# Two transformer layers on one core: feature sums on TensorE, small products on GpSimd, a first chunk normalised tile by tile, and an order written out as a table

## The chip, the cores and the metric

The kernel is one program on one core of a Trainium2 chip. A core has TensorE (matrix products; PE in the profile, and PEld for its weight loads), VectorE (DVE), ScalarE (ACT), GpSimd (POOL) and SyncE (SP), which run their own instruction streams in order and wait for each other by semaphores. In this kernel SyncE and, at the start, ScalarE issue the DMA transfers. The metric is the device time of one execution in microseconds. Lower is better.

## The reference

A sequence of 2048 rows of 512 bfloat16 values goes through an attention layer (A) and a gated feed-forward layer (B), twice, with the same weights both times:

```python
def _A_ref(x, wqkv, w_phi, wo):            # H = 32 heads of Dh = 16
    q, k, v = ...                          # from x @ wqkv
    pq = jnp.einsum("bhsd,hdf->bhsf", q, w_phi)
    pk = jnp.einsum("bhsd,hdf->bhsf", k, w_phi)
    phi_q = jnp.concatenate([_softmax(pq), _softmax(-pq)], axis=-1)
    phi_k = jnp.concatenate([_softmax(pk), _softmax(-pk)], axis=-1)
    kv = jnp.einsum("bhsf,bhsd->bhfd", phi_k, v)
    z  = jnp.einsum("bhsf->bhf", phi_k)
    num = jnp.einsum("bhqf,bhfd->bhqd", phi_q, kv)
    den = jnp.einsum("bhqf,bhf->bhq", phi_q, z)[..., None] + 1e-6
    return (num / den) ... @ wo
def _B_ref(x, W_gate, W_up, W_down):       # F = 1376
    gate, up = x @ W_gate, x @ W_up
    return ((gate * (gate > 0)) * up) @ W_down
x = x + _A_ref(_layernorm(x), ...)
x = x + _B_ref(_layernorm(x), ...)         # and both once more
```

The attention is linear: keys and values are first summed over all 2048 rows into one small matrix for each head, and only then can the queries be applied.

## The kernel before

The 2048 rows are 16 tiles of 128, in four chunks of four tiles. X stays in the core's memory for the whole run. For each chunk and layer the stages are these.

**Normalisation** (class `Norm`, line 367). The statistics of a tile come either from VectorE (`bn_stats` at L385, aggregated at L387), or from sums: the addition that makes the new X also accumulates its row sum (L494), and ScalarE accumulates the squares (L408). GpSimd makes the inverse standard deviation with a few tiny instructions (L393 to L444). ScalarE (L456), VectorE or GpSimd (both L468) scales the tile. The scaled tile is then transposed, either by a DMA transpose that SyncE issues, one tile at a time (L486) or a pair of tiles (L482), or on TensorE (L477) with a copy out of PSUM (L304 on ScalarE, L306 on VectorE). `groups` says how many tiles share the tiny instructions; for the first chunk it is (1, 1, 2), and `turn` ("A---") has tile 0 alone turned on TensorE.

**Weights of the features** (`feature_weights`). `w_phi` is folded into the key and query weights: the key weights are transposed on TensorE (L348), multiplied (L361) and copied out (L304, L306); the query weights are transposed by two DMA transposes (L334).

**Keys and values** (`keys_values`, `values`). For each tile four matmuls give the features (L637) and four the values (L590). ScalarE takes exp of the features and of their negatives (L642). `feature_sums` adds up each head's 16 exponentials of either sign: in one VectorE reduction (L609), in two halves (L619), or with a first addition on GpSimd (L606) and the rest on VectorE (L615). VectorE inverts the sums (L651); GpSimd, VectorE or both multiply (L657); eight matmuls of 68 columns add the tile into the key-value sums (L679). VectorE then spreads those sums into the matrix R (L701).

**Queries and attention** (`queries`, `attention`). Four matmuls (L721), two exps (L725), the sums as above, a reciprocal (L730) and a small product (L732), both on VectorE, a scale of half of the tile (L739), a DMA transpose (L741), eight matmuls against R (L758), a division (L776, L778), a transpose (DMA at L785 and L791, or TensorE at L798) and the output projection (L809).

**Feed-forward** (`glu`). For each chunk matmuls with the gate and the up weights (L540, and L520 for the last 96 columns), evacuation by ScalarE and VectorE, and eleven matmuls for each tile of the result (L572). Other weights than those of keys, values and queries are loaded by SyncE, piece by piece (`load_weights`, L297).

The **order** on every engine is made when the program is built. Each operation is recorded with an engine, a duration and what it reads and writes (`Plan.op`); loads carry an earliest time (`at`), which is known to the planner only. `Plan.order` then goes through a planned time and gives each free engine the ready operation with the highest rank, which is the longest chain behind it plus a bias from the table `RANK`. Operations are emitted in that order, and at run time each engine keeps to it, waiting on semaphores for data and for buffers. There are six PSUM buffers of the kind `ps` (`KINDS`). Strings in `STEP`, one letter per tile, choose among the variants: `kr` and `qr` the way of the feature sums for keys and queries ("1" one reduction, "2" two, "P" and "H" with GpSimd), `qs` and `ks` who scales, `xn`, `xB` and `xA` who normalises, `ev` who evacuates values, with the layer behind the name.

Of the kernel before, what the change touches and what calls it, by code (L numbers as in the profile page):

```python
# [60 lines left out]
class Plan:  # L61
# [10 lines left out]
    def op(self, eng, occ, fn, reads=(), writes=(), holds=(), lat=0.0, at=0.0, group=None, port=False, long=False):  # L72
# [4 lines left out]
        base, slope = RANK.get(f"{o.group}.{eng}") or RANK[o.group]  # L77
        o.bias = base - slope * o.i_in
# [19 lines left out]
    def order(self):  # L98
        for o in self.ops:
            for p in o.preds:  # L100
                p.succs.append(o)
        for o in reversed(self.ops):
            o.rank = o.cost + o.lat + max([s.rank + hop(o.eng, s.eng) for s in o.succs], default=0.0)
        free = {k: [0.0] * n for k, (pool, n) in self.kinds.items()}
        engines = sorted({o.eng for o in self.ops})
        busy = {e: 0.0 for e in engines}
        ready = {e: [] for e in engines}
        for o in self.ops:
            o.wait, o.t0 = len(o.preds), o.at
            if not o.wait:  # L110
                ready[o.eng].append(o)
        seq, left, now, shut = [], len(self.ops), 0.0, 0.0
        while left:
            moved, later = False, []
            for e in engines:
                if busy[e] > now + 1e-9:
                    later.append(busy[e])
                    continue
                best = None
                for o in ready[e]:  # L120
                    if o.t0 > now + 1e-9:
                        later.append(o.t0)
                        continue
                    if o.port and shut > now + 1e-9:
                        later.append(shut)
                        continue
                    ok = True
                    need = {}
                    for b in o.bufs:
                        if b.slot is None:  # L130
                            need[b.kind] = need.get(b.kind, 0) + 1
                    for k, n in need.items():
                        got = [t for t in free[k] if t is not None]
                        if len(got) < n:
                            ok = False
                        else:
                            t = sorted(got)[n - 1]
                            if t > now + 1e-9:
                                later.append(t)
                                ok = False  # L140
# [792 lines left out]
```

## Time and profile before

| | |
|---|---|
| median of three runs | 382.85 us (381.29 to 383.61) |
| the profiled execution | 380.87 us |
| its span, first to last instruction | 379.1 us |
| TensorE busy | 368.0 us, 97%, 2435 matmuls |
| VectorE, ScalarE, GpSimd busy | 272.1, 211.0 and 139.5 us |
| mean granted clock of TensorE | 0.995 |

The times of instructions come from one profiled execution, which has a time of its own; the median is that of three others. A matmul's busy time includes the time that its result takes to drain, so consecutive matmuls overlap: four of 512 columns take about 0.86 us when others follow. In a timeline row the columns are the start and the length in us, the engine and line, the operation, output and inputs, and in brackets the engine's idle time before it and what ended it. In a row of groups stand the busy time in us and the mean of one in ns, then the idle time before them. In the table by stretches each engine has its busy us and its instructions; PEclk is the granted clock as a share of full speed, then the busy share of the DMA engines and GB/s. A row of the DMA view gives an issue's count, size and us from issue to landing.

### The profile page before, as it was taken

The page shows a single profiled execution, that of the slowest core. Times are in us where ns is not written, and L with a number is a line of the kernel's source. Part 1 is how long each engine was busy: PE and PEld are TensorE (multiplying, and loading weights), DVE is VectorE, ACT ScalarE, POOL GpSimd, SP SyncE. Part 2 cuts the span into 40 slices and gives each one's busy share as a digit, 9 for nine tenths or more (in the row PEclk, how much of TensorE's full clock was granted, in tenths as well). Part 3 has the DMA queues.
Part 4 walks back from the last instruction along what each step waited for, and adds up shares of the span by engine and source line. Part 5 has one row for each costly group of instructions (what it writes and reads, how often), then busy time and mean ns, then how long its engine had stood idle before and what let it go on. Part 6 is the DMA issues. An engine that isn't in the chain of part 4 may idle for free.

```text
span 379.1 us, 6873 instructions
## 1 busy us (share of the span) xinstructions
PE 368.0 (97%) x2435; PEld 190.8 (50%) x2435; DVE 272.1 (72%) x606; ACT 211.0 (56%) x436; POOL 139.5 (37%) x272
## 2 busy tenths in 40 slices
PE   8699999999999999999999999999999999999996
PEld 4245545666445454444454455576655444454444
DVE  5999999999789725636992688999985592532232
ACT  4899878752598241238476377986725135124600
POOL 3799876903366000134360446545311021000000
PEclk9899999999999999999999999999999999999999
DMA  8999816449585100141232020656977014020011
GB/s 255 252 219 212 211 39 138 47 91 173 96 153 100 29 15 2 28 57 29 47 52 55 3 55 2 124 104 86 164 153 112 0 28 112 0 28 30 1 43 55
DMA packets 98403, 32.23 MB, mean 85 GB/s; under 512 B 88800, under 2 KB 98368, under 8 KB 98368
## 3 DMA queue, kind: packets, MB, share of 16 engines
q1 hardware_dynamic: 94400, 28.36, 39.8%
q10 hardware_dynamic: 3968, 3.42, 2.9%
q8 instruction: 19, 0.31, 0.4%
q14 instruction: 16, 0.13, 0.1%
HBM read 8.44 MB, written 2.10 MB: 28 GB/s over the span
## 4 chain that ended last, share of the span: by engine, by line
PE 80%; DVE 9%; DMA 4%; POOL 4%; issue 1%; SPq 1%; ACT 0%; ACTq 0%; POOLq 0%
PE ps L540 36%; PE ps L572 19%; PE ps L809 6%; PE ps L721 4%; PE ps L590 4%; PE ps L637 3%; DMA b<-b 3%; PE ps L520 3%; PE q L758 2%; DVE sk L619 2%; POOL b L657 1%; PE ps L315 1%; DVE rk L651 1%; PE q L679 1%; DVE bnst L385 1%
## 5 line engine op out<-in xcount | busy, mean ns | idle before, releaser
L540 PE MATMUL ps<-b,wu 128*128 128x512 bf16 (+2 forms) x400 | 79.4, 337 | 0.0
L540 PE MATMUL ps<-b,wg 128*128 128x512 bf16 (+2 forms) x400 | 78.9, 337 | 0.0
L572 PE MATMUL ps<-wd,b 128*128 128x512 bf16 (+3 forms) x374 | 78.3, 367 | 0.0
L550 ACT CAST b<-ps 128x512 bf16<-128x512 f32 (+2 forms) x100 | 48.9, 505 | 40.6 <-PE ps L540 39.3
L553 DVE SCALAR_TENSOR_TENSOR b<-ps,b 128x512 bf16<-128x512 f32 (+2 forms) x60 | 34.9, 598 | 30.3 <-PE ps L540 29.8
L572 PEld LDWEIGHTS <-b 128*128 128x128 bf16 (+1 forms) x374 | 35.3, 98 | 39.4
L657 POOL TENSOR_TENSOR b<-b,rk 128x1024 bf16<-128x1024 bf16 (+6 forms) x30 | 42.1, 1410 | 33.9 <-DVE rk L651 26.0
L540 PEld LDWEIGHTS <-wg 128*128 128x128 bf16 x400 | 36.2, 98 | 32.9 <-issue 0.2
L540 PEld LDWEIGHTS <-wu 128*128 128x128 bf16 x400 | 36.1, 98 | 31.9
L456 ACT ACTIVATE b<-X,ve,rstd 128x512 bf16<-128x512 bf16 x42 | 33.4, 818 | 26.2 <-POOL ve L444 21.5
L739 POOL TENSOR_TENSOR b<-b,rq 128x512 bf16<-128x512 bf16 x25 | 26.3, 1050 | 31.2 <-DVE rq L732 24.2
L498 DVE TENSOR_TENSOR X<-X,ps 128x512 bf16<-128x512 bf16 (+2 forms) x34 | 22.0, 649 | 21.2 <-PE ps L572 20.6
L725 ACT ACTIVATE b<-ps 128x512 bf16<-128x512 f32 x64 | 33.3, 615 | 6.2 <-PE ps L721 6.1
L408 ACT ACTIVATE sq<-X 128x512 bf16<-128x512 bf16 x32 | 20.0, 626 | 28.5 <-DVE X L494 26.2
L637 PE MATMUL ps<-Wk,b 128*128 128x512 bf16 x128 | 31.5, 388 | 4.0 <-DMA b<-b 4.0
L642 ACT ACTIVATE b<-ps 128x512 bf16<-128x512 f32 x64 | 33.2, 612 | 1.2 <-PE ps L637 1.2
L494 DVE SCALAR_TENSOR_TENSOR X<-ps,X 128x512 bf16<-128x512 f32 x32 | 21.7, 684 | 13.4 <-PE ps L572 12.5
L809 PE MATMUL ps<-wo,b 128*128 128x512 bf16 x128 | 30.9, 379 | 0.1
L590 PE MATMUL ps<-wkv,b 128*128 128x512 bf16 x128 | 30.9, 384 | 0.0
L721 PE MATMUL ps<-Wq,b 128*128 128x512 bf16 x128 | 30.9, 379 | 0.0
L557 DVE TENSOR_TENSOR b<-b,b 128x512 bf16<-128x512 bf16 (+2 forms) x40 | 14.1, 373 | 22.3 <-ACT b L550 21.9
L546 ACT ACTIVATE b<-ps 128x512 bf16<-128x512 f32 (+2 forms) x40 | 19.8, 496 | 15.1 <-PE ps L540 15.1
(84 smaller groups left out, 463.8 us busy)
## 6 DMA issues: line engine op xcount, KB each, us to landing
out_dram<-X SPq DMA_DIRECT2D x15, 128.0 KB, 1.7
X<-in_A_x_dram ACTq DMA_DIRECT2D x3, 512.0 KB, 7.6
b<-b SPq DMA_TRANSPOSE x87, 3.2
wd<-in_B_W_down_dram SPq DMA_DIRECT2D x5, 256.0 KB, 3.2
wu<-in_B_W_up_dram SPq DMA_DIRECT2D x8, 160.0 KB, 3.3
wg<-in_B_W_gate_dram SPq DMA_DIRECT2D x8, 160.0 KB, 2.9
wkv<-in_A_wqkv_dram ACTq DMA_DIRECT2D x2, 512.0 KB, 5.1
wq<-in_A_wqkv_dram ACTq DMA_DIRECT2D x1, 512.0 KB, 8.3
```

Of the source, the lines that this page charges most:

```text
L456: pl.op("ACT", 0.72, lambda to=to, t=t, j=j: nc.scalar.activation(out=to(), in_=st.X[:, t, :], func=AF.Identity, scale=rstd[:, j:j + 1], b ...
L540: nc.tensor.matmul(ps[:], lhsT=wt[:, b, f * P:(f + 1) * P], rhs=xnT[:, lo:hi, b, :], start=(b == 0), stop=(b == NDB - 1))
L550: pl.op("ACT", 0.065 + 0.42 * share, lambda ups=ups, ru=ru: nc.scalar.copy(out=ru[:], in_=ups[:]), reads=[(ups, 0)], writes=[(ru, 0)])
L553: pl.op("DVE", 0.08 + 0.53 * share, lambda gps=gps, ru=ru, h=h, cs=cs: nc.vector.scalar_tensor_tensor(out=h[:, cs], in0=gps[:], scalar=0.0 ...
L572: nc.tensor.matmul(yps[:], lhsT=hs[f][:fsz, ti * P:(ti + 1) * P], rhs=st.wd[:fsz, f, cols], start=(f == 0), stop=(f == NFT - 1))
L590: nc.tensor.matmul(vp[:], lhsT=xnT[:, ti, kb, :], rhs=st.wkv[:, kb, D:2 * D], start=(kb == 0), stop=(kb == NDB - 1))
L637: nc.tensor.matmul(ps[:], lhsT=xnT[:, ti, kb, :], rhs=w(kb), start=(kb == 0), stop=(kb == NDB - 1))
L642: pl.op("ACT", 0.49, lambda s=s, ek=ek, pk=pk: nc.scalar.activation(out=ek[:, :, s, :], in_=pk[:].rearrange("p (j x) -> p j x", j=8), func ...
L657: eng.tensor_tensor(out=phiK[:, lo:hi, :, :].rearrange("p j s (f h) -> p (j s) f h", h=4), in0=ek[:, lo:hi, :, :].rearrange("p j s (f h) - ...
L721: nc.tensor.matmul(pq[:], lhsT=xnT[:, ti, kb, :], rhs=st.Wq2[:, kb, :], start=(kb == 0), stop=(kb == NDB - 1))
L725: pl.op("ACT", 0.49, lambda s=s, eq=eq, pq=pq: nc.scalar.activation(out=eq[:, :, s, :], in_=pq[:].rearrange("p (j x) -> p j x", j=8), func ...
L809: nc.tensor.matmul(yps[:], lhsT=turned(b), rhs=st.wo[:, b, :], start=(b == 0), stop=(b == NDB - 1))
```

## The change

1. `feature_sums` gets a way "T". The tile of exponentials is transposed by a DMA transpose on SyncE, and eight matmuls with a 0/1 matrix of eight columns (`M8s`) add up its features into PSUM. The reciprocal then reads PSUM. The table uses it for key tiles 0, 2, 4, 6, 9 and 11 of the first layer.
2. A string `qm` says for each query tile whether the small product runs on VectorE or GpSimd; 20 of 32 are on GpSimd.
3. The first chunk is normalised in groups (1, 1, 1, 1), and `turn` is "ADDD": all four tiles are transposed on TensorE, and VectorE copies three of them out.
4. Other strings of `STEP` change: who scales, evacuates and normalises, which chunks take their statistics from sums, which tiles are transposed in pairs. In the second layer's B stage three tiles of a chunk were turned on TensorE, now one.
5. `Plan.order` no longer searches. It reads the order of all 1891 operations from the table `ORDER`, and `RANK` goes. Some planned durations and arrival times are changed; they have no effect at run time but through that table.

The computed function stays the same. The diff, cut to its core:

```diff
     def order(self):
-        ... (the search by rank)
         free = {k: [0.0] * n for k, (pool, n) in self.kinds.items()}
+        busy, shut, seen = {}, 0.0, set()
+        assert sorted(ORDER) == list(range(len(self.ops)))
+        self.seq = [self.ops[i] for i in ORDER]
+        for o in self.seq:
+            assert o.preds <= seen
+            seen.add(o)
...
-WF_IN, WK_IN, WV_IN, WQ_IN, LOADED = 3.5, 5.9, 8.6, 13.1, 13.0
-X_IN = [3.25, 3.8] + [7.0] * 2 + [10.1] * 4 + [11.6] * 4 + [14.5] * 4
+WF_IN, WK_IN, WV_IN, WQ_IN, LOADED = 3.4, 6.05, 8.25, 12.75, 13.0
+X_IN = [3.25, 4.55] + [6.75] * 2 + [9.75] * 4 + [11.25] * 4 + [14.2] * 4
...
+    st.M8s = const.tile([P, 2, 4], BF16, name="M8s")
+    nc.vector.tensor_reduce(out=st.M8s[:], in_=ident[:].rearrange("p (z k h) -> p z h k", z=2, h=4), axis=AX.X, op=Alu.max)
...
+    if how == "T":
+        turned = Buf("b2", [P, 8, P], BF16)
+        pl.op("SP", 1.25, lambda: nc.sync.dma_start_transpose(out=turned[:], in_=e[:].rearrange("p j s x -> p (j s x)")),
+              reads=[(e, 0), (e, 1)], writes=[(turned, 0)], lat=2.0, group=(group, t))
+
+        def add_up():
+            for j in range(8):
+                nc.tensor.matmul(sums[:, j, :, :].rearrange("p s h -> p (s h)"), lhsT=turned[:, j, :],
+                                 rhs=st.M8s[:].rearrange("p s h -> p (s h)"), start=True, stop=True)
+        pl.op("PE", 0.26, add_up, reads=[(turned, 0)], writes=[(sums, 0), (sums, 1)], group=(group, t))
+        return
...
+        how = STEP["qr" + L][t]
+        sums = Buf("ps", [P, 8, 2, 4], F32) if how == "T" else sq2
+        feature_sums(st, how, eq, sums, "f" + L, "i" + L, t)
...
+        by_pool = STEP["qm" + L][t] == "P" and how != "T"
+        pl.op("POOL" if by_pool else "DVE", 0.23 if by_pool else 0.19, lambda sq2=sq2, sums=sums, rq=rq, by_pool=by_pool: (
+            nc.gpsimd if by_pool else nc.vector).tensor_tensor(out=rq[:], in0=sq2[:, :, 1, :], in1=sums[:, :, 0, :], op=Alu.mult),
+            reads=[(sq2, 1), (sums, 0)], writes=[(rq, 0)])
...
-    "part0": "4111", "part1": "4111", "tB0": "A---", "tB1": "D-DA", "tA": "----", "wev": "AADDAAADADAAAAAA",
+    "part0": "4111", "part1": "4111", "tB0": "A---", "tB1": "---A", "tA": "----", "wev": "AAADDAADAADDAAAA",
...
-    "xn1": "AAAAADAPDAADAADA", "turn": "A---", "wake": 17, ..., "sB0": 3, "sB1": 2, "sA": 3,
+    "xn1": "DADDADAPDAADAADA", "turn": "ADDD", "wake": 19, ..., "sB0": 4, "sB1": 4, "sA": 2,
...
-    "kr0": "H1111P1121221222", "kr1": "P12111111H12P222",
+    "kr0": "T1T1TPT12T1T1222", "kr1": "12P121211222P221", "qm0": "DDDDPPPPPDPPPPDP", "qm1": "PDDPDPPDPPPPDPPD",
...
-RANK = {...}
+ORDER = (
+    128, 129, 142, 137, 139, 125, 140, 133, 132, 135, 136, 130, 126, 127, 143, 0, 1, 2, 3, 144, 7, 4, 8, 145, 5,
...
-        n = Norm(st, "b4", (1, 1, 2) if c == 0 else (2, 2), STEP["xn1"], STEP["xm0"], X_IN, STEP["turn"] if c == 0 else "")
+        n = Norm(st, "b4", (1, 1, 1, 1) if c == 0 else (2, 2), STEP["xn1"], STEP["xm0"], X_IN, STEP["turn"] if c == 0 else "")
```

In the program built from the changed kernel, SyncE's first instructions are the two loads of X, one load each of up, gate and down weights, the transpose for tile 0's sums, the transpose of the tile pair 4 and 5, another load, a transpose of query weights, the pair 6 and 7, the other transpose of query weights, and the transpose for tile 2's sums. In the kernel before they are the two loads of X, the transpose of tile 1, a load of down weights, the pair 2 and 3, the pair 4 and 5, and the two of query weights.

127 lines of the change are left out of this document (30 added, 97 removed), and 125 rows, old and new, of tables (ORDER, RANK, STEP).

## The prediction

> **What bounds the kernel now.** I read the page's totals first, then the table by stretches, then the TensorE timeline of the start, then the chain of waits of the first layer.
>
> ```profile
> span 379.1 us, 6873 instructions
> PE 368.0 (97%) x2435; PEld 190.8 (50%) x2435; DVE 272.1 (72%) x606; ACT 211.0 (56%) x436; POOL 139.5 (37%) x272
> ```
> ```profile
> core 0: us, PE busy (x) PEld busy (x) DVE busy (x) ACT busy (x) POOL busy (x), PEclk, DMA share, GB/s
> 0.00:6.60 6.60, 5.36 (x16) 2.02 (x17) 3.60 (x14) 1.49 (x2) 2.77 (x17) 1.00 0.72 209
> 6.60:14.50 7.90, 4.85 (x49) 3.04 (x47) 6.37 (x18) 7.38 (x14) 4.21 (x13) 1.00 1.08 330
> 14.50:19.30 4.80, 4.47 (x14) 1.51 (x15) 4.80 (x15) 3.35 (x6) 4.44 (x8) 0.64 0.92 184
> 19.30:30.00 10.70, 9.90 (x78) 5.17 (x77) 9.84 (x20) 10.03 (x20) 10.38 (x16) 1.00 1.14 223
> 30.00:54.00 24.00, 23.32 (x197) 12.03 (x195) 23.38 (x42) 21.03 (x41) 20.92 (x16) 1.00 0.63 156
> 54.00:71.00 17.00, 15.75 (x129) 8.25 (x127) 16.91 (x43) 14.96 (x31) 12.42 (x20) 1.00 0.47 93
> 71.00:110.00 39.00, 38.20 (x318) 23.15 (x315) 35.15 (x97) 19.81 (x53) 17.13 (x45) 1.00 0.71 119
> 110.00:285.00 175.00, 174.89 (x1169) 91.18 (x1168) 132.12 (x291) 102.81 (x223) 62.05 (x126) 1.00 0.37 64
> ```
>
> TensorE is the bound: from 110 to 285 us it is idle for 0.11 us of 175. So the end moves by two things only: matmul work added or taken away, and TensorE idle time in the first 110 us. From 19.3 to 71 us that idle time is 0.80 + 0.68 + 1.25 = 2.73 us, and VectorE is busy for 50.13 of 51.7 us there, so it sets that idle time; 71 to 110 has 0.80 more. The start is where most is lost:
>
> ```profile
> 6.59 1.06 PE L348 MATMUL ps<-ident,wkv 128*128 128x128 bf16 x16
> ...
> 9.47 1.03 PE L590 MATMUL ps<-wkv,b 128*128 128x512 bf16 x4
> 10.43 1.02 PE L637 MATMUL ps<-Wk,b 128*128 128x512 bf16 x4
> 14.54 1.04 PE L637 MATMUL ps<-Wk,b 128*128 128x512 bf16 x4 [3.09 <-DMA b<-b]
> 15.41 1.55 PE L590 MATMUL ps<-wkv,b 128*128 128x512 bf16 x4
> 17.25 4.57 PE L637 MATMUL ps<-Wk,b 128*128 128x512 bf16 x16 [0.29 <-DMA b<-b]
> 21.66 0.39 PE L679 MATMUL q<-vext,b 128*128 128x68 bf16 x7
> ```
>
> After tile 0, TensorE waits 3.09 us for the DMA transpose of tile 1. Then four matmuls take 1.55 us in place of 1.03: the clock is 0.64 of full in that stretch (table above), so 4.80 x 0.36 = 1.7 us of it is lost. By 21.66 TensorE has done eight groups of four for keys and values.
>
> **The change, part by part.** Rows for its prices:
>
> ```profile
> 10.21 1.25 DVE L385 BATCH_NORM_STATS2 bnst<-X 128x6 f32<-128x512 bf16 x2
> 11.38 0.16 DVE L387 BATCH_NORM_AGGREGATE mv<-bnst 128x2 f32<-128x6 f32 x1
> ```
> ```profile
> L468 DVE TENSOR_SCALAR b<-X,mv,rstd 128x512 bf16<-128x512 bf16 x7 | 2.8, 408 | 1.9 <-POOL rstd L395 1.9
> L306 DVE COPY b<-ps 128x512 bf16<-128x512 bf16 x8 | 3.1, 402 | 1.8 <-PE ps L348 1.8
> L306 DVE CAST Wk<-ps 128x512 bf16<-128x512 f32 x1 | 0.7, 673 | 0.0
> L306 DVE CAST vext<-ps 128x512 bf16<-128x512 f32 x3 | 2.0, 679 | 0.0
> L609 DVE TENSOR_REDUCE sk<-b 128x64 f32<-128x1024 bf16 x16 | 19.0, 1195 | 3.8 <-ACT b L642 3.8
> L619 DVE TENSOR_REDUCE sk<-b 128x32 f32<-128x512 bf16 x24 | 15.2, 658 | 0.4 <-ACT b L642 0.4
> L615 DVE TENSOR_REDUCE sk<-b 128x32 f32<-128x256 f32 x8 | 4.5, 568 | 0.2 <-POOL b L606 0.2
> L732 DVE TENSOR_TENSOR rq<-sq 128x32 bf16<-128x32 f32 x32 | 9.0, 282 | 0.1
> L730 DVE RECIPROCAL sq<-sq 128x32 f32<-128x32 f32 x32 | 10.8, 337 | 0.0
> L776 DVE RECIPROCAL dd<-q 128x32 f32<-128x32 f32 x32 | 10.9, 340 | 0.8 <-PE q L758 0.7
> L444 POOL TENSOR_TENSOR ve<-u,rstd 128x2 f32<-128x2 f32 x24 | 4.7, 197 | 1.2
> ```
>
> First, **the first chunk tile by tile**, with all four tiles turned on TensorE. No DMA transpose stands ahead of tiles 1 to 3 any more; VectorE's own order does. It reads, in the changed program: the copy of a turned weight block (0.40), statistics of tiles 2 and 3 (1.25, with two aggregations of 0.16), two key-weight casts (2 x 0.67), statistics of 4 and 5 (1.25), a scaling (0.41), two aggregations, a scaling (0.41), the copy of tile 1. TensorE's weight transposes end at 7.65, as before; the copy starts at 7.5. So the casts end at 7.5 + 0.40 + 1.25 + 0.32 + 1.35 = 10.8, and tile 0's keys run then and not at 10.43. Tile 1 is copied out at 10.8 + 1.25 + 0.41 + 0.32 + 0.41 + 0.40 = 13.6, against 14.54 now. The next tile needs 1.25 + 0.32 + 0.41 + 0.40 more (16.0), the last 1.25 + 0.40 (17.65). Each gives TensorE two groups, 1.73 us at full clock (15.41 less 14.54 for one group), which fit between those times: it has done eight groups at 17.65 + 0.15 + 1.73 = 19.5, not 21.66. **Gain 2.15 us**, the twelve transposes included, since they run in gaps. The longest gap left is about 1.4 us (12.2 to 13.6), so I count no slow clock; if it came back, it would cost 1.7 us of this.
>
> [...]
>
> Second, **sums on TensorE** for key tiles 0, 2, 4, 6, 9 and 11 of the first layer: 48 matmuls of 8 columns, each with a 128x128 weight load. No row has 8 columns; the nearest has 68:
>
> ```profile
> 40.17 1.23 PE L679 MATMUL q<-vext,b 128*128 128x68 bf16 x33
> ```
>
> Less the 0.19 us that one takes to drain, these start every 1.04/32 = 32 ns, each with its own weight load. Between nothing (in idle time) and the 56 ns of a 128-column transpose (1.06 us less 0.22 over 15), I take 32: 48 x 0.032 = **1.55 us added**, ends 0 and 2.7. VectorE loses four whole reductions (1.19), one split pair (0.66 + 0.57) and two halves (0.66): 7.3 us. It keeps the reciprocal, now from PSUM; the two reciprocal rows (0.337 from SBUF, 0.340 from PSUM) price that at nothing. The sums hold one of the six PSUM buffers until that reciprocal; hidden while VectorE isn't late, and if it is, a delay of up to one reduction, 1.2 us, for the matmul that wants the buffer.
>
> Third, **small products on GpSimd**: 20 of 32, ten in the first layer. VectorE sheds 0.28 each. GpSimd's nearest row has two columns for 32 and takes 0.20; I take 0.25, so 2.5 us in the first layer, beside 3.1 + 4.6 us of GpSimd's idle time between 30 and 71 us (table). Mostly they stand just ahead of a scale on GpSimd that waits for them anyway; without that cover each delays one query tile by 0.25 us.
>
> Fourth, **the planner's order becomes a table and options move**. VectorE gains, ahead of the first feed-forward matmul: three scalings and three copies (2.4), a key-weight cast (0.67), two value casts (1.36), one whole-tile scale (about 0.8) and a small mask (0.27), 5.5 us together. With 7.3 less and some five products (1.4) gone, about 3 us net leave a stretch in which VectorE is full. I let that remove half of the 2.73 us of TensorE idle time: **1.4 us**, ends 0 and 2.73. Half and not all, because GpSimd and SyncE release TensorE there too. In the second layer two tiles fewer are turned on TensorE (8 x 56 ns): **0.45 us less**. The two added dummy matmuls fill gaps. Statistics that move to ScalarE (eight more squares) and scalings that leave it (13) lie beside a full TensorE.
>
> Sum: -2.15 + 1.55 - 1.4 - 0.45 = **-2.45 us**. The profiled execution took 380.87 us (span 379.1 and 1.8 around it), which gives 378.4. The median of the runs shown, 382.85, is 0.52% above that execution, so I state 380.4 on its scale: 0.64% less.
>
> **The rivals.** *SyncE's queue becomes the bound (slower).* Its rows:
>
> ```profile
> 11.11 1.29 SPq L486 DMA_TRANSPOSE b<-b  x1
> 12.46 0.57 SPq L297 DMA_DIRECT2D wd<-in_B_W_down_dram  x1
> 14.00 2.62 SPq L482 DMA_TRANSPOSE b<-b  x2
> 16.71 2.67 SPq L334 DMA_TRANSPOSE b<-wq  x2
> ```
> ```profile
> X<-in_A_x_dram ACTq DMA_DIRECT2D x1, 256.0 KB, 4.7
> b<-b SPq DMA_TRANSPOSE x87, 3.2
> b<-wq SPq DMA_TRANSPOSE x2, 4.2
> ```
> ```profile
> L468 POOL TENSOR_SCALAR b<-X,mv,rstd 128x512 bf16<-128x512 bf16 x1 | 2.1, 2096 | 0.1
> ```
>
> A DMA transpose holds the queue for 1.3 us, lands 3.2 us after its issue, and early, beside other traffic, 4.2. Six are added (7.8 us of queue) and two go (tile 1's, and the pair's). In the new order the transpose for tile 2's sums stands behind two tile pairs, a load and both query-weight transposes. Of these the second pair waits for GpSimd's normalisation (2.1 us), to about 18.7; with 1.3 for that pair, 1.3 for the weights and 0.6 of slips it issues near 21.9 and lands at 25.1 to 26.1. TensorE comes to it after six more groups and some small ones, near 25.4. Behind it stand transposes of tiles 8 to 15 and, in TensorE's order, everything else. So a landing over about 3.5 us decides: then TensorE waits for the queue, up to 7.8 - 2.6 = 5.2 us, and no idle time is won: 380.87 - 2.15 + 1.55 - 0.45 + 5.2 = 385.0, on the median's scale 387.0 (+1.1%). For it: the early landings; against: most landings are 3.2, and VectorE's work ahead shrinks too.
>
> *The start doesn't get earlier.* The planner holds weight loads back to 13 us, but that is a number of the plan; in the program nothing makes them wait. In the changed order three of them (160 + 160 + 256 KB) stand on SyncE ahead of its first transpose, so they issue at about 1.7 us and share the engines with the loads of X that ScalarE issued (tiles 2 and 3, 256 KB, land 4.7 us after their issue). At the 330 GB/s of the second stretch 576 KB take 1.8 us. Tiles 2 to 7 then land up to 1.8 us later, and the statistics that VectorE runs ahead of its casts and scalings wait. If all of that reaches TensorE, 0.4 us of the 2.15 is left, nothing is won later, and the time is 380.87 - 0.4 + 1.55 - 0.45 = 381.6, or 383.5. VectorE has work until 7.9 anyway, so I expect 0.1 to 0.5 us of it.
>
> [...]
>
> *All idle time goes (faster).* If VectorE alone made the 2.73 + 0.80 us between 19.3 and 110, less work there wins it all: 380.87 - 2.15 + 1.55 - 0.45 - 3.5 = 376.3, or 378.3 (-1.2%). For it: VectorE is busy for 16.91 of 17.0 us before the first feed-forward stage. Against: TensorE's own work ahead of that stage grows by some 2 us.
>
> **How the numbers follow.** One per cent is about what a measurement of this kernel can tell from no change. Forecast 0.44, all idle gone 0.28, SyncE's queue 0.21, the start no earlier 0.07. The range takes the low case less another 2 us (sums in idle time cost nothing, an earlier start) and the slow case plus 0.5: 376 to 387.5. The forecast's centre lies 1.4 us above the 1% line at 379.0, so a fifth of it counts as faster: faster 0.37, within 1% 0.42, slower 0.21.
>
> **What will show it.** Tile 1's value and key matmuls near 13.6 us with the clock at 1.00 up to 20 us; eight groups done by 19.5. The 48 small matmuls at about 32 ns with no idle time before the first of each eight; idle time there, released by a DMA transpose, is SyncE's rival. Loads of wu, wg and wd issued before 4 us, with over 6 us in place of 4.7 for tiles 2 and 3 to land, are the third case. TensorE idle of 1 to 2 us between 19.3 and 71 is the forecast, under 0.5 the fast rival. I would be wrong altogether if new waits appeared after 110 us, where every order is new and TensorE has nothing to win.

## The result and the profile after

The changed kernel takes 385.61 us (median of 14 runs, 383.99 to 388.85) beside 382.63 us for the kernel before, run with it (14 runs, 381.29 to 383.61): a ratio of 1.0083, 95% interval 1.0061 to 1.0106. It is slower by 0.8%, within the 1% but on the other side of zero than forecast. The profiled execution took 385.5 us, its span 383.4 us, 4.3 more than before; the timed runs lose less, about 3.2 us, since the profiled execution of the kernel before (380.87) was a short one. Line numbers below are those of the changed kernel: key features L595, values L536, exps L600, one reduction L566, halves L576, reciprocal L609, scale of keys L615, key-value sums L637, the new matmuls L561, small product L694, scale of queries L701, R L659. Some of the edits below insert lines, which shifts these numbers a little.

The page's totals of the changed kernel:

```profile
span 383.4 us, 6914 instructions
PE 370.0 (96%) x2489; PEld 191.9 (50%) x2489; DVE 273.1 (71%) x605; ACT 199.3 (52%) x433; POOL 134.9 (35%) x286
```

The same stretches as in the prediction, of the changed kernel:

```profile
core 0: us, PE busy (x) PEld busy (x) DVE busy (x) ACT busy (x) POOL busy (x), PEclk, DMA share, GB/s
...
14.50:19.30 4.80, 4.66 (x22) 1.97 (x21) 4.80 (x15) 3.85 (x7) 4.07 (x9) 1.00 0.83 169
19.30:30.00 10.70, 9.26 (x69) 4.57 (x68) 9.54 (x20) 9.80 (x20) 9.55 (x16) 1.00 1.10 180
30.00:54.00 24.00, 22.06 (x230) 12.34 (x228) 22.74 (x38) 19.45 (x38) 19.52 (x15) 1.00 0.77 171
54.00:71.00 17.00, 14.87 (x114) 7.63 (x115) 16.96 (x39) 12.13 (x25) 12.16 (x20) 1.00 0.69 138
71.00:110.00 39.00, 38.46 (x325) 23.25 (x324) 35.80 (x94) 18.90 (x54) 19.34 (x53) 1.00 0.58 113
110.00:285.00 175.00, 173.91 (x1149) 90.11 (x1148) 135.33 (x293) 97.31 (x218) 57.27 (x131) 1.00 0.37 63
```

The clock stays at 1.00 in the start, where it had been 0.64. But from 19.3 to 71 us TensorE is idle for 1.44 + 1.94 + 2.13 = 5.51 us, where it had been 2.73. The start itself went as forecast; TensorE's timeline:

```profile
13.84 1.04 PE L536 MATMUL ps<-wkv,b 128*128 128x512 bf16 x4
14.71 2.21 PE L595 MATMUL ps<-Wk,b 128*128 128x512 bf16 x8
16.75 1.03 PE L536 MATMUL ps<-wkv,b 128*128 128x512 bf16 x4
17.62 1.03 PE L595 MATMUL ps<-Wk,b 128*128 128x512 bf16 x4
18.48 1.03 PE L536 MATMUL ps<-wkv,b 128*128 128x512 bf16 x4
19.34 0.34 PE L561 MATMUL ps<-M8s,b 128*128 128x8 bf16 x8
```

To see where that gain goes, I add up, up to each point of time, the time less the matmuls that compute something, each counted with the time from its start to the next one's where they follow each other at full clock (0.216 us for 512 columns, 0.032 for 68, 0.025 for 8). What is left is what TensorE has lost by then, in us:

| up to | before | changed | e1 | e9 | e14 |
|---|---|---|---|---|---|
| 19.3 us | 12.31 | 9.48 | 9.70 | 9.70 | 9.28 |
| 71 us | 16.19 | 16.35 | 14.02 | 15.01 | 13.37 |
| 230 us | 17.56 | 17.93 | 15.77 | 16.85 | 14.66 |
| 250 us | 17.87 | 19.46 | 17.26 | 18.17 | 15.94 |
| 300 us | 18.37 | 20.87 | 17.85 | 19.36 | 16.56 |

(e1, e9 and e14 are experiments below.) The change is 2.83 us ahead at 19.3 us and 0.16 behind at 71; it loses 0.2 more up to 230, 1.2 between 230 and 250 and 0.9 by 300. With 1.42 us of added matmul work and 0.35 of a longer tail behind the last matmul that makes the 4.3 us.

The largest single loss is a wait for the last key tile's scale, in TensorE's timeline:

```profile
50.50 2.20 PE L637 MATMUL q<-vext,b 128*128 128x68 bf16 x56
54.95 0.43 PE L637 MATMUL q<-vext,b 128*128 128x68 bf16 x8 [2.26 <-POOL b L615]
```

GpSimd made that scale late because its reciprocal came late. GpSimd's timeline:

```profile
36.31 11.71 POOL L615 TENSOR_TENSOR b<-b,rk 128x1024 bf16<-128x1024 bf16 x7 [0.81 <-DVE rk L609]
50.19 1.91 POOL L615 TENSOR_TENSOR b<-b,rk 128x1024 bf16<-128x1024 bf16 x1 [2.17 <-DVE rk L609]
52.98 1.91 POOL L615 TENSOR_TENSOR b<-b,rk 128x1024 bf16<-128x1024 bf16 x1 [0.89 <-DVE rk L609]
```

And the reciprocals were late because VectorE stood in two scales ahead of them, of 128x128 and 128x640:

```profile
44.40 0.54 DVE L609 RECIPROCAL rk<-ps 128x64 bf16<-128x64 f32 x1
44.97 3.40 DVE L615 TENSOR_TENSOR b<-b,rk 128x128 bf16<-128x128 bf16 x2
48.29 1.27 DVE L576 TENSOR_REDUCE sk<-b 128x32 f32<-128x512 bf16 x2
49.48 0.54 DVE L609 RECIPROCAL rk<-sk 128x64 bf16<-128x64 f32 x1
```

In the kernel before the same two scales take 0.60 us together, and a third one 0.15:

```profile
46.02 0.60 DVE L657 TENSOR_TENSOR b<-b,rk 128x128 bf16<-128x128 bf16 x2
46.54 1.27 DVE L619 TENSOR_REDUCE sk<-b 128x32 f32<-128x512 bf16 x2
47.73 0.54 DVE L651 RECIPROCAL rk<-sk 128x64 bf16<-128x64 f32 x1
48.19 0.15 DVE L657 TENSOR_TENSOR b<-b,rk 128x128 bf16<-128x128 bf16 x1
```

Taken one by one, the changed kernel's two run from 44.97 to 46.45 and from 46.37 to 48.37; GpSimd's operations beside them end at 46.36 and 48.02. Before, they began at 46.02 and 46.13, when GpSimd's operation was ending (46.13), and the third fell between two of GpSimd's. There the second scale was ahead of GpSimd's next one, and GpSimd's took longer: begun at 46.18, its 128x896 took 1.99 us, where the other five of that kernel took 1.69 to 1.77. So the theory, **A**: a VectorE scale that comes up while GpSimd runs one of its own stands until GpSimd is done, and the table puts three of them where GpSimd runs without a gap. Rivals: VectorE is simply full; GpSimd is too slow; the turned sums, the products on GpSimd or the start are what costs.

### The profile page after: what moved, and what is told of

Its sections match the earlier page's. It is cut to its first block, busy times and chain, and to the rows that moved or that the text cites. A ratio compares the mean times of both kernels' runs of the same rounds, so it can differ in the third digit from the quotient of the medians.

```text
span 383.4 us, 6914 instructions
## 1 busy us (share of the span) xinstructions
PE 370.0 (96%) x2489; PEld 191.9 (50%) x2489; DVE 273.1 (71%) x605; ACT 199.3 (52%) x433; POOL 134.9 (35%) x286
## 4 chain that ended last, share of the span: by engine, by line
PE 74%; DVE 12%; DMA 8%; ACT 2%; issue 2%; POOL 1%; SPq 0%; DVEq 0%; POOLq 0%
PE ps L486 34%; PE ps L518 18%; DMA b<-b 8%; PE ps L771 6%; PE ps L679 3%; PE ps L595 3%; PE ps L466 2%; DVE b L615 2%; PE q L720 2%; DVE sk L576 2%; PE ps L536 2%; PE ps L261 2%; DVE rk L609 1%; DVE sq L566 1%; ACT b L600 1%
## 5 line engine op out<-in xcount | busy, mean ns | idle before, releaser
L496 ACT CAST b<-ps 128x512 bf16<-128x512 f32 (+2 forms) x100 | 47.4, 505 | 79.2 <-PE ps L486 68.1
L518 PE MATMUL ps<-wd,b 128*128 128x512 bf16 (+4 forms) x374 | 79.4, 366 | 0.0
L615 POOL TENSOR_TENSOR b<-b,rk 128x1024 bf16<-128x1024 bf16 (+7 forms) x29 | 37.7, 1313 | 19.6 <-DVE rk L609 12.1
L600 ACT ACTIVATE b<-ps 128x512 bf16<-128x512 f32 x64 | 35.7, 607 | 13.0 <-PE ps L595 12.6
L683 ACT ACTIVATE b<-ps 128x512 bf16<-128x512 f32 x64 | 34.4, 608 | 13.0 <-PE ps L679 12.8
L354 ACT ACTIVATE sq<-X 128x512 bf16<-128x512 bf16 x40 | 25.3, 633 | 24.4 <-DVE X L440 23.9
L595 PE MATMUL ps<-Wk,b 128*128 128x512 bf16 x128 | 31.9, 379 | 1.9 <-DMA b<-b 1.0
L402 ACT ACTIVATE b<-X,ve,rstd 128x512 bf16<-128x512 bf16 x29 | 23.8, 819 | 17.0 <-POOL ve L390 16.8
L440 DVE SCALAR_TENSOR_TENSOR X<-ps,X 128x512 bf16<-128x512 f32 x40 | 26.5, 679 | 7.6 <-PE ps L771 5.9
L536 PE MATMUL ps<-wkv,b 128*128 128x512 bf16 x128 | 31.7, 379 | 0.0
L361 POOL TENSOR_SCALAR u<-mv 128x2 f32<-128x2 f32 (+1 forms) x24 | 5.7, 241 | 72.2 <-DVE X L440 71.5
L444 DVE TENSOR_TENSOR X<-X,ps 128x512 bf16<-128x512 bf16 (+2 forms) x26 | 16.2, 638 | 17.8 <-PE ps L518 17.7
L701 POOL TENSOR_TENSOR b<-b,rq 128x512 bf16<-128x512 bf16 x19 | 20.0, 1062 | 14.5 <-ACT b L492 9.4
```

The source lines that it names most:

```text
L440: pl.op("DVE", 0.61, lambda: nc.vector.scalar_tensor_tensor(out=st.X[:, t, :], in0=yps[:], scalar=1.0, in1=st.X[:, t, :], op0=Alu.mult, op ...
L496: pl.op("ACT", 0.065 + 0.42 * share, lambda ups=ups, ru=ru: nc.scalar.copy(out=ru[:], in_=ups[:]), reads=[(ups, 0)], writes=[(ru, 0)])
L518: nc.tensor.matmul(yps[:], lhsT=hs[f][:fsz, ti * P:(ti + 1) * P], rhs=st.wd[:fsz, f, cols], start=(f == 0), stop=(f == NFT - 1))
L536: nc.tensor.matmul(vp[:], lhsT=xnT[:, ti, kb, :], rhs=st.wkv[:, kb, D:2 * D], start=(kb == 0), stop=(kb == NDB - 1))
L595: nc.tensor.matmul(ps[:], lhsT=xnT[:, ti, kb, :], rhs=w(kb), start=(kb == 0), stop=(kb == NDB - 1))
L600: pl.op("ACT", 0.49, lambda s=s, ek=ek, pk=pk: nc.scalar.activation(out=ek[:, :, s, :], in_=pk[:].rearrange("p (j x) -> p j x", j=8), func ...
```

## The experiments

| run | median us | ratio to before, 95% interval |
|---|---|---|
| e1_scales_on_pool | 381.92 | 0.9979 [0.9963, 0.9995] |
| e1d_scales_on_dve | 384.07 | 1.0043 [1.0026, 1.0061] |
| e3_no_turned_sums | 390.57 | 1.0203 [1.0180, 1.0227] |
| c0_after_again | 384.77 | 1.0073 [1.0049, 1.0096] |
| e2_both_layers | 381.72 | 0.9989 [0.9966, 1.0012] |
| e4d_products_on_dve | 390.77 | 1.0214 [1.0181, 1.0246] |
| e6_start_undone | 386.24 | 1.0108 [1.0073, 1.0143] |
| e9_order_only | 382.45 | 1.0015 [0.9999, 1.0031] |
| e12_order_both_layers | 382.67 | 1.0018 [1.0000, 1.0036] |
| e6b_start_undone_no_lock | 383.91 | 1.0046 [1.0029, 1.0063] |
| e5_loads_later | 385.04 | 1.0073 [1.0045, 1.0101] |
| e14_loads_in_gap | 379.82 | 0.9944 [0.9922, 0.9966] |
| e15_loads_and_layer2 | 379.74 | 0.9937 [0.9912, 0.9961] |

**The disputed cost by itself.** A program of its own: VectorE runs an operation once alone and once just after GpSimd has begun a scale of 1.91 us. Its core (a, r and f lie in SBUF, rp in PSUM):

```diff
+    for k, test in enumerate(tests):
+        for beside in (0, 1):
+            d = marker(f"{k}a{beside}")
+            if beside:
+                nc.gpsimd.tensor_scalar_mul(out=gr[:].rearrange("p j s h -> p (j s h)"), in0=d[:], scalar1=1.0)
+                scaled(nc.gpsimd, pool.tile([P, 8, 2, 64], BF16, name=f"o{k}"), g, gr, 0, 8)
+            marker(f"{k}b{beside}")
+            marker(f"{k}c{beside}")
+            test(f"t{k}_{beside}")
...
```

> This kernel computes nothing of the reference: it copies the input to the output and runs ten VectorE operations twice each, once with GpSimd idle and once while one of GpSimd's scales of 128x1024 (1.91 us in the changed kernel) is running. Theory A (a VectorE operation that reads both inputs from SBUF can't run beside a GpSimd operation): the scales of 128x128 and 128x640 with both inputs in SBUF, which take about 0.2 and 0.43 us alone, the product of 128x32 and the 128x512 product take over 1 us longer beside GpSimd and end within 0.1 to 0.4 us of GpSimd's end; the reduction, and the operations with one input in PSUM, take the same time in both. Rival (VectorE's long scales at 45 to 48 us waited for their own data or a semaphore, not for GpSimd): every operation takes the same time in both, within 0.1 us.

VectorE's timeline; of each pair the second stands beside GpSimd:

```profile
5.13 0.16 DVE L52 TENSOR_TENSOR t<-a,r 128x128 bf16<-128x128 bf16 x1
...
6.48 1.79 DVE L52 TENSOR_TENSOR t<-a,r 128x128 bf16<-128x128 bf16 x1
...
15.04 0.76 DVE L52 TENSOR_TENSOR t<-a,rp 128x640 bf16<-128x640 bf16 x1
...
17.00 0.76 DVE L52 TENSOR_TENSOR t<-a,rp 128x640 bf16<-128x640 bf16 x1
...
29.80 1.16 DVE L68 TENSOR_REDUCE t<-a 128x64 f32<-128x1024 bf16 x1
...
32.16 1.16 DVE L68 TENSOR_REDUCE t<-a 128x64 f32<-128x1024 bf16 x1
...
35.53 0.31 DVE L70 TENSOR_SCALAR t<-X,stat 128x512 bf16<-128x512 bf16 x1
...
37.05 1.93 DVE L70 TENSOR_SCALAR t<-X,stat 128x512 bf16<-128x512 bf16 x1
```

GpSimd's first scale in the same program:

```profile
6.28 1.91 POOL L52 TENSOR_TENSOR o<-g,gr 128x1024 bf16<-128x1024 bf16 x1
```

The scale of 128x128 ends at 8.27, 0.08 us after GpSimd's at 8.19. The one of 128x640 goes from 0.43 to 2.13 us, the small product of 128x32 from 0.13 to 1.83, a product of two 128x512 tiles from 0.36 to 2.06. With one input in PSUM nothing changes (0.76 and 0.76; the small product 0.13 and 0.13; an addition 0.63 and 0.63), and the reduction doesn't change either (1.16 and 1.16). A normalising scale of 128x512, which has one large input in SBUF, is held too (0.31 to 1.93). Theory A holds for what it says of scales and products; why the normalising scale is held as well and the reduction, also with one large input in SBUF, is not, no run here shows.

**The scales taken away from VectorE, and given to it.** In e1 GpSimd does all of tiles 11 to 13, in e1d VectorE does (letter "D"):

```diff
         deps = [(ek, 0), (ek, 1), (rk, 0)]
+        if (L, t) in WHOLE:
+            def scale(eng, lo, hi, one=scale, todo=[WHOLE[L, t]]):
+                if todo:
+                    one(nc.gpsimd if todo.pop() == "P" else nc.vector, 0, 8)
...
+WHOLE = {('0', 11): 'P', ('0', 12): 'P', ('0', 13): 'P'}
```

> Layer 1's key tiles 11, 12 and 13 are scaled by GpSimd alone (8 blocks each in place of 7, 3 and 7); VectorE's three scales (128x128, 128x640, 128x128) go. GpSimd gets 7 blocks more, about 1.6 us. Theory A: VectorE no longer stands from 44.97 to 48.29 us, the reciprocal of the last key tile comes some 3 us earlier, GpSimd runs without the gaps of 2.17 and 0.89 us, its last scale ends at about 53.4 in place of 54.89 us, and TensorE's stall of 2.42 us at 52.5 shrinks by about 1.5: total -1.0 to -1.7 us, 384.0 to 384.7. Rival B (the last sums are late for another reason: GpSimd's throughput or the transposes for the key sums): GpSimd has more to do, so the stall grows by up to 1.6 us: 385.5 to 387.2.

> The opposite shift: layer 1's key tiles 11, 12 and 13 are scaled by VectorE alone (8 blocks each in place of 1, 5 and 1), and GpSimd's scales of 7, 3 and 7 blocks go, 4.2 us of its time. Theory A: with no GpSimd operation beside them the three scales take about 0.6 us each, 1.8 in place of 3.9 us, the last key tile's scale on GpSimd ends at about 52.7 in place of 54.89 us, and the stall of 2.42 us at 52.5 goes nearly altogether: total -1.5 to -2.4 us, 383.2 to 384.1. Rival B (VectorE is simply full, its own work being the bound): 14 more blocks are 1.0 us more on VectorE: 385.6 to 386.6.

Both shifts gain, though they load opposite engines: 1.04% and 0.40% of the time less than the changed kernel, 4.0 and 1.5 us. In e1 GpSimd runs through, and TensorE's last wait is shorter (the timelines of GpSimd and TensorE in e1):

```profile
42.03 11.27 POOL L615 TENSOR_TENSOR b<-b,rk 128x1024 bf16<-128x1024 bf16 x6
53.48 2.06 POOL L705 TENSOR_TENSOR b<-b,rq 128x512 bf16<-128x512 bf16 x2 [0.18 <-issue]
```
```profile
53.36 0.43 PE L641 MATMUL q<-vext,b 128*128 128x68 bf16 x8 [0.89 <-POOL b L615]
```

The last key sums come 1.59 us earlier, as A had it. The total gained more than the 1.0 to 1.7 that I gave it: 0.73 us of TensorE's wait at 59.3 us goes as well, and a wait at 288 us that has another cause (below). GpSimd's throughput as the bound falls: it got 1.6 us more work in e1 and the time fell. A VectorE that is simply full falls too, by e1d: it got 17 blocks more (not 14, as I wrote), about 1.2 us at their length when nothing holds them, and the kernel got faster; the three scales took 2.65 us there, less than the 4.0 of the three held ones.

**Only the order.** The decisive run: no operation changes its engine; three rows of the table move.

```diff
-        self.seq = [self.ops[i] for i in ORDER]
+        moved = [294, 305, 317]
+        rows = [i for i in ORDER if i not in moved]
+        rows[rows.index(337) + 1:rows.index(337) + 1] = moved
+        self.seq = [self.ops[i] for i in rows]
...
-         ("mv", 12), ("ve", 4), ("u", 4), ("sq", 1), ("rstd", 12), ("sk", 4), ("rk", 4), ("dd", 4))
+         ("mv", 12), ("ve", 4), ("u", 4), ("sq", 1), ("rstd", 12), ("sk", 4), ("rk", 6), ("dd", 4))
```

> No work changes its engine: in the table three rows are moved, VectorE's scales of layer 1's key tiles 11, 12 and 13 (128x128, 128x640, 128x128), from ahead of the last two tiles' reductions and reciprocals to behind them; the ring of reciprocals gets 6 buffers in place of 4, since they live longer. Theory A (VectorE stands at a scale that GpSimd's scale blocks, and the reductions queued behind it start late): the reductions start at 44.97 in place of 48.29 us, GpSimd's scales follow each other without gaps and the last ends at about 52 in place of 54.89 us, VectorE's three scales are still stretched by GpSimd but nothing waits behind them; TensorE's stall of 2.42 us at 52.5 shrinks by 1.4 or more: ratio 0.998 to 1.002 (after: 1.0083 and 1.0073), 381.5 to 383.0. Rival H (e1_scales_on_pool gained because 0.8 us of work left a full VectorE, wherever it stood): 1.006 to 1.010, 384.5 to 386.1.

VectorE's timeline in e9, where reductions and reciprocals now come first:

```profile
45.63 1.28 DVE L579 TENSOR_REDUCE sk<-b 128x32 f32<-128x512 bf16 x2 [0.56 <-ACT b L603]
46.83 0.54 DVE L612 RECIPROCAL rk<-sk 128x64 bf16<-128x64 f32 x1
...
49.34 0.50 DVE L612 RECIPROCAL rk<-sk 128x64 bf16<-128x64 f32 x1
49.75 0.36 DVE L618 TENSOR_TENSOR b<-b,rk 128x128 bf16<-128x128 bf16 x1
```

The ratio is 1.0015, where the changed kernel had 1.0083 and 1.0073: 2.2 to 2.6 us from the order of three operations. The 128x640 scale is still held (50.03 to 52.25 us), but no reduction of a key tile waits behind it, and GpSimd ends its last scale at 51.91. The rival, that e1 gained by the 0.8 us of work that left VectorE, gave 1.006 to 1.010 and falls. Nor is it the two added buffers: in the changed kernel VectorE has no idle time ahead of a reciprocal between 39 and 56 us. This answers where most of the loss comes from: 2.2 to 2.6 of the 2.8 to 3.2 us by which the timed runs of the changed kernel are slower than the kernel before.

**The parts of the change, undone one at a time.** The sums back on VectorE:

```diff
-        pl.op("SP", 1.25, lambda: nc.sync.dma_start_transpose(out=turned[:], in_=e[:].rearrange("p j s x -> p (j s x)")),
+        pl.op("SP", 1.25, lambda: None,
...
-            for j in range(8):
-                nc.tensor.matmul(sums[:, j, :, :].rearrange("p s h -> p (s h)"), lhsT=turned[:, j, :],
-                                 rhs=st.M8s[:].rearrange("p s h -> p (s h)"), start=True, stop=True)
+            nc.vector.tensor_reduce(out=sums[:].rearrange("p j s h -> p (j s) h"),
+                                    in_=e[:].rearrange("p j s (f h) -> p (j s) h f", h=4), axis=AX.X, op=Alu.add)
```

> The six key tiles' sums go back to VectorE (one reduction of 128x1024 each, about 1.17 us), written to the same PSUM tile at the place of TensorE's 48 matmuls; the six DMA transposes and the 48 matmuls go. Theory A (VectorE is what the stage up to 71 us lacks): 7.0 us more on an engine that is busy 22.74 of the 24 us from 30 to 54, less 1.2 us of matmuls: +3 to +6 us, 388.5 to 391.5. Rival C (the transposed copies are what costs: 1.2 us of matmuls, the transposes' landings and SyncE's queue): -1 to -3 us, 382.5 to 384.5.

1.2% slower than the changed kernel, some 4.6 us. The turned sums are no cause of the loss; in this table they are worth that much. The small products back on VectorE:

```diff
-        ... lambda sq2=sq2, sums=sums, rq=rq, by_pool=by_pool: (
+        ... lambda sq2=sq2, sums=sums, rq=rq, by_pool=False: (
```

> All small query products (128x32) back on VectorE; the rest as in the changed kernel. Theory A: each goes to the engine that GpSimd's scales block, 0.13 to 0.18 us alone and up to 1.8 beside a scale; about twenty more of them: +0.3 to +2.0 us, 385.7 to 387.4. Rival D (the products on GpSimd are what makes the change slow, by standing behind GpSimd's scales): -0.5 to -2 us, 383.4 to 384.9. My own prediction took the move for free: 0.

1.3% slower, 5 us, more than I gave it. The products themselves are hardly held (0.18 us at the median; three of 32 took 0.45 to 1.09). More than half of the loss, 3.7 of the 6.1 us between the two profiles, is one place in layer 2, TensorE's timeline in e4d:

```profile
285.80 3.62 PE L518 MATMUL ps<-wd,b 128*128 128x512 bf16 x16
292.13 1.04 PE L771 MATMUL ps<-wo,b 128*128 128x512 bf16 x4 [2.71 <-DMA b<-b]
```

In the changed kernel GpSimd makes the last product of the chunk itself at 274.75 us and its two scales follow at 275.08 and 276.09. In e4d the two products stand behind a division on VectorE, at 284.60 and 284.70; GpSimd's two scales come at 284.86 and 285.87, SyncE issues the two query transposes at 285.94 and 287.28 instead of 277.76 and 279.1, and the transpose for the output projection stands behind them in its queue. That is read from one profile and not tested further. The table was also made for products on GpSimd, so this run doesn't show what a table made for them on VectorE would cost; the same holds for the sums in e3.

The start undone, in the changed kernel and in e1 (the three copies out of PSUM go too):

```diff
...
+                by_dma = self.at is not None and t > 0
+
-                def turn(tp=tp, xn=xn):
+                def turn(tp=tp, xn=xn, ti=ti, by_dma=by_dma):
+                    if by_dma:
+                        return nc.sync.dma_start_transpose(out=self.dst[:, ti, :, :], in_=xn[:])
...
```

> Tiles 1 to 3 of the first chunk are turned by the DMA queue, as before the change, in place of TensorE and the evictions; the rest as in the changed kernel. If the 2.83 us that the start had gained at 19.3 us reach the end: +2 to +3 us, 387.4 to 388.4, with R as much later than 58.04 us. Rival G (what VectorE and GpSimd do between 30 and 55 us sets R's time whatever the start does): R within 0.5 us of 58.04, total within 0.7 us of 385.4.

> e1_scales_on_pool with tiles 1 to 3 of the first chunk turned by the DMA queue again. To be compared with e1_scales_on_pool (ratio 0.9979). If the start's gain (2.83 us at 19.3 us) counts in full once VectorE's stand is gone: +2 to +3 us, ratio 1.003 to 1.006. Rival G (it is swallowed later in any case, as e6_start_undone against the changed kernel showed 1.0108 against 1.0083 and 1.0073): +0.7 to +1.3 us, ratio 0.9995 to 1.0015.

In the changed kernel the undone start costs only 0.0025 to 0.0035 of the ratio, about 1.1 us, with wide intervals. In e1 it costs 0.0067, or 2.6 us (1.7 to 3.4 by the two intervals): no loss of the start's gain shows there, and my guess G, that later stages would swallow it (+0.7 to +1.3 us), is out. (The profiled execution of e6b, the shortest of its runs, is only 0.7 us longer than that of e1; the timed runs decide.) Both runs undo more than the turning: the three weight loads now stand behind the transposes of tiles 1 to 3, are issued after 14 us, and X's last tiles land 1.7 us earlier (14.24 in e6b, 15.97 in e1). So the turning alone may be worth more.

**Weight loads ahead of the first transpose.**

```diff
+        moved = [113, 105, 122]
+        rows = [i for i in ORDER if i not in moved]
+        rows[rows.index(163) + 1:rows.index(163) + 1] = moved
...
```

> e1_scales_on_pool with the three weight loads (wu, wg, wd) that SyncE issued at 1.71, 2.18 and 2.65 us moved behind the transposes of the query weights, at about 16 us. My rival 'start doesn't get earlier' said that they make X's tiles land up to 1.8 us later. If so, tiles 2 to 15 land 0.5 to 1.8 us earlier and the waits for them in the first 20 us shrink: ratio 0.994 to 0.997. If the transfers were not in each other's way: landings within 0.2 us, ratio 0.997 to 0.999.

X did land earlier: its last four tiles at 14.41 us instead of 15.97, and at 19.3 us TensorE had lost 8.42 instead of 9.70. But the time rose by 3.6 us. The three loads were issued at 21.53 to 22.63 us (not at about 16, as I wrote), just ahead of the transpose for tile 2's sums; that one was issued at 23.16, took 4.04 us to land, and TensorE waited for it (its timeline in e5):

```profile
25.00 0.38 PE L644 MATMUL q<-vext,b 128*128 128x68 bf16 x7
27.25 0.35 PE L564 MATMUL ps<-M8s,b 128*128 128x8 bf16 x8 [1.87 <-DMA b<-b]
...
28.30 1.69 PE L598 MATMUL ps<-Wk,b 128*128 128x512 bf16 x4 [0.42 <-DMA b<-b]
29.78 1.91 PE L539 MATMUL ps<-wkv,b 128*128 128x512 bf16 x4
```

After that wait four matmuls of 512 columns take 1.7 to 1.9 us and not 1.03. The stretch shows why:

```profile
28.30:31.90 3.60, 3.60 (x9) 1.29 (x10) 1.97 (x5) 1.78 (x3) 3.38 (x4) 0.53 1.09 192
```

The granted clock was 0.53. So the same loads went into a stretch where SyncE issues nothing (the diff is that of e5 with row 100 in place of 163), and, in e15, layer 2's last key tiles onto VectorE as well:

> e1_scales_on_pool (ratio 0.9979) with the three weight loads of 1.71 to 2.65 us moved to SyncE's empty stretch behind the load of 46.52 us. In e5_loads_later X's tiles landed 1.5 us earlier and the start was 1.28 us ahead at 19.3 us, but the loads, now at 15.8 to 24 us between the transposes, made a transpose late (1.9 us of TensorE's wait at 25.19). If that collision was the whole loss: X's tiles land 1.5 us earlier again, the wait at 25 us is gone, and 0.8 to 1.3 us are left at the end: ratio 0.9945 to 0.996. If the earlier start itself is what upsets the stage (the same table meets other times): a new stall by 60 us, ratio 0.998 to 1.004.

> e14_loads_in_gap with layer 2's key tiles 13, 14 and 15 scaled by VectorE alone, as in e2_both_layers. TensorE's stalls for those sums were 1.26 us in e1_scales_on_pool and 0.69 in e2_both_layers, but the total didn't show it (0.9989 against 0.9979, intervals overlapping). If the 0.6 us count: ratio 0.0015 below that of e14_loads_in_gap. If they are made up for behind (the same work waits later): within 0.0007 of it.

Without the collision nothing of e5's loss is left, and the earlier landings (the last four tiles at 14.13 us) are worth 0.0035 against e1, 1.3 us (0.3 to 2.4 by the two intervals). Both versions beat the kernel before, e15 by 0.6% (0.4 to 0.9). That is as much as the prediction forecast (0.64%), but for kernels that place the scales and three loads otherwise than the change did.

**Layer 2's last key sums.** The 1.2 us lost between 230 and 250 us are of the same kind: VectorE's scales at 233.66 and 235.47 take 1.15 us each and end 0.3 us after GpSimd's. TensorE's timeline in the changed kernel:

```profile
235.60 0.30 PE L637 MATMUL q<-vext,b 128*128 128x68 bf16 x4 [0.26 <-DVE b L615]
236.32 0.68 PE L637 MATMUL q<-vext,b 128*128 128x68 bf16 x8 [0.42 <-POOL b L615]
```

e2, e12 and e15 give tiles 13 to 15 of layer 2 to VectorE, on top of e1, e9 and e14.

```diff
+WHOLE = {..., ('1', 13): 'D', ('1', 14): 'D', ('1', 15): 'D'}
```

> Key tiles 11 to 13 of layer 1 on GpSimd as in e1_scales_on_pool, and beside that layer 2's key tiles 13, 14 and 15 scaled by VectorE alone (8 blocks each, GpSimd's 4, 4 and 3 blocks go). To be compared with e1_scales_on_pool (ratio 0.9979). Theory A: VectorE's two scales of 1.15 us at 231.6 and 233.4 become 0.6 us, TensorE's three stalls there (0.43, 0.59 and 0.24 us) shrink by 0.5 to 1.0: ratio 0.995 to 0.9966, 380.3 to 380.9. Rival B (VectorE is full there, its own work bounds): 11 blocks more on VectorE, 0 to +0.8 us: ratio 0.998 to 1.000.

> e9_order_only and, beside it, layer 2's key tiles 13, 14 and 15 scaled by VectorE alone as in e2_both_layers. Theory A: as e9_order_only and 0.3 to 0.7 us less, ratio 0.996 to 1.000. Rival: the same ratio as e9_order_only.

TensorE's stalls there fell from 1.26 to 0.69 us in the profile of e2, but the ratios moved by +0.0010, +0.0003 and -0.0007. That these stalls count at the end is not shown; an effect of 0.6 us is less than the intervals are wide.

**The wait at 288 us.** TensorE's timeline in the changed kernel, and the answer for L432, whose two transposes were issued at 283.78 and 285.06:

```profile
287.65 1.02 PE L771 MATMUL ps<-wo,b 128*128 128x512 bf16 x4
289.71 1.89 PE L486 MATMUL ps<-b,wu 128*128 128x512 bf16 x8 [1.04 <-DMA b<-b]
```
```profile
L432 SPq DMA_TRANSPOSE b<-b x2: 1188/1202/1217, 283.8 to 285.1; - x2
...
DMA to landing us min/median/max: 2.4/3.5/4.5
```

> The changed kernel once more, unedited, beside the next three. Theory F (its stall of 1.2 us at 288.3, behind a DMA transpose that took 4.52 us while a fetch of instructions was under way, is a coincidence of one execution): the profile has no such stall at that place, and its span is about 1.2 us shorter, 382.2. Rival (it belongs to the kernel): the stall is there again.

The wait was there again (0.68 us at 289.0), so it belongs to the kernel; "coincidence of one execution" was wrong. What it goes with is a fetch of instructions, 16 KB on a queue of its own:

| | second transpose of the pair, issued | landed after | the fetch began |
|---|---|---|---|
| changed | 285.06 | 4.52 | 286.3 |
| changed again | 285.76 | 4.00 | 287.7 |
| e9 | 283.65 | 4.34 | 285.9 |
| e5 | 285.23 | 3.80 | 286.4 |
| e1 | 283.20 | 2.45 | 287.1 |
| e1d | 284.58 | 2.45 | 288.4 |
| e2 | 282.59 | 2.45 | 286.6 |
| e12 | 284.82 | 2.45 | 288.8 |

Where the fetch began within 2.3 us of the issue, the transpose took 3.8 to 4.5 us and TensorE waited 0.5 to 1.2 us; where it began later, 2.45 us and no such wait. In four more profiles that have this pair (e6, e6b, e14, e15) it began 3.8 to 4.7 us after the issue, and the transpose landed after 2.43 to 2.45 us. No run moved the fetch alone, so that it causes the delay is argued from twelve profiles and not tested.

## Why the prediction was wrong

Term by term, from the table of what TensorE has lost, with the added matmul work put to its terms: the start -2.16 us (forecast -2.15), the sums +1.2 (+1.55), the second layer's transposes -0.45 (-0.45), 19.3 to 71 us +3.0 (-1.4), 71 us to the end +2.3 (nothing), the tail +0.35 (nothing). That is 4.2 of the 4.3 us between the two profiles. So the two terms that failed are the idle time that was to go, and the waits put at nothing.

**The start: right.** Eight groups of keys and values were done by 19.34 us (forecast 19.5), tile 1 began at 13.84 (13.6), the clock stayed up (1.00 from 14.5 to 19.3 us). That a gap of 1.4 us would leave it up was my estimate and wasn't put to the test: from 6.6 to 19.3 us TensorE's longest wait was 0.64 us. The 2.83 us of the table don't count the twelve added transposes; less their 0.67 us the gain is 2.16, and 2.15 was forecast with them. Between e1 and e6b it is 2.6 us of the total (1.7 to 3.4).

**Sums on TensorE: right, a little dear.** Eight matmuls take 0.34 us, less the 0.17 that a single one takes: 0.17/7 = 24 ns each and not 32, so about 1.2 us and not 1.55. All added matmul work, 1.42 us, is 1.2 plus the start's twelve transposes (0.67) less the eight that the second layer sheds (0.45). Waits ahead of the new matmuls were small, 0.48 us at the longest.

**The small products: too little.** I counted what VectorE sheds (1.4 us, in the 3 net) and nothing for GpSimd. Undone, in a table made for the move, they cost 5 us, more than half of it, by one profile, where a product late on VectorE made GpSimd and SyncE late. A move's worth isn't the time of the moved operation.

**The planner's order and the options: this step failed.** I let VectorE "shed about 3 us net" and turned that into 1.4 us less of TensorE's idle time between 19.3 and 71 us. The idle time rose by 2.78 us. VectorE's busy time in that stretch fell only from 50.13 to 49.24 us, because its scales and products stood 3.8 us longer beside GpSimd than before (operations longer by more than 0.2 us than the shortest of their kind, up to 75 us: 5.56 us too long in all, 1.77 before). The work did leave: without the 3.8 us it would have been 4.7 us less. I took durations as properties of operations and VectorE's load as their sum. What it cost that three of these scales stood ahead of the key tiles' reductions is shown by e9: 2.2 to 2.6 us, with the same work on the same engines. The mean of the small products that I quoted, 282 ns, already held the sign: alone one takes 0.13 us (m0_lock_alone), and the median of those 32 is 0.18. The code said it too: `Plan.op` marks scales as `port` or `long`, and `order` holds a `port` operation back while a `long` one runs. The small products carry neither mark. I described the order and passed these words by.

**Waits after 110 us: named, not priced.** I wrote that I would be wrong altogether if they appeared. They did: 1.09 us of idle time from 110 to 285 us in place of 0.11, and the 1.04 us at 289. They are about 2 of the 4.3 us, though no run here shows how much of them is left at the end, and what makes the one at 289 is argued above, not tested.

**The rivals.** SyncE's queue as the bound was priced at 387.0, near the result, but for the wrong reason: the transposes for the sums hardly make TensorE wait, and without them (e3) the kernel is slower. A part of it came true: a transpose of a tile pair that stood in that queue until 19.11 us landed at 23.50, and TensorE lost 1.2 us there. "The start doesn't get earlier" had a right mechanism, X's tiles landing 1.6 us later behind the three loads (e1 against e5; I said up to 1.8), and a wrong consequence, since the start gained all the same; undone it is worth about 1.3 us (e14). That all idle time goes was the furthest off. No rival had two engines getting in each other's way.

## What to carry to other kernels

An operation's length can depend on what runs beside it (the scale of 128x128 took 0.16 us alone and 1.79 beside GpSimd's): before adding up a full engine's load, look in the trace for one operation with two lengths, and at what ends together with the long ones. An engine that keeps to a fixed order can't step aside when its next operation is held; put operations that may be held behind those for which others wait (worth 2.2 to 2.6 us in e9), or give one input from PSUM: none of the three such operations in the program of its own was held (0.76, 0.13 and 0.63 us, alone and beside GpSimd). When a transfer is moved, look at the stretch that it moves into as closely as at the one that it leaves.

## What was unexpected in the hardware

VectorE's normalising scale of 128x512, with a single large input in SBUF, is held by GpSimd as fully as a product with two (0.31 to 1.93 us, against 0.36 to 2.06 for the product of two 128x512 tiles).

DMA transposes land later beside an instruction fetch in the whole trace, not only at 288 us. In the changed kernel a fetch of 16 KB began within 2.2 us of the issue of 19 of them (the shortest takes 2.28 us to land); they landed after 4.13 us on average, the other 89 after 3.04. In the kernel before it was 14 after 3.78 and 85 after 3.06. That the fetch is the cause isn't shown.

TensorE's clock fell to 0.53 in e5 (28.30 to 31.90 us) after a wait of 1.87 us with only small matmuls around it, while in the changed kernel it stayed at 1.00 (55.2 to 59 us) behind a wait of 2.26 us. Between these two the length of the gap did not decide; what did isn't shown.
